# Sliding-window and linear attention side by side: v's weights loaded by parts of the contraction, an output projection moved, and the last rows stored in halves

## The chip, the cores and the metric

The kernel runs on one core of a Trainium2 chip. The time is in device microseconds; the medians below are over three runs. The profile is of one further execution, whose own time stands beside its span. Engines are named as in the profile: PE multiplies matrices, PEld loads its weights, DVE, ACT and POOL work on vectors, SP issues the DMA transfers here.

## What is computed

Two attention blocks of the same size on two inputs of 2048 tokens by 640 columns, 32 heads of 20, all in bfloat16. A is softmax attention in which a query sees itself and the 255 tokens before it. B is linear attention with phi(t) = t + 1 for positive t and exp(t) otherwise. Their outputs stand side by side in the result's columns.

```
qkv = x @ wqkv                      # both
A: s = q k^T * 20**-0.5, masked to 0 <= i - j < 256
   o = softmax(s) v ;  out[:, 0:640]    = o @ wo
B: kv = sum_s phi(k) v^T ;  z = sum_s phi(k)
   o = phi(q) kv / (phi(q) z + 1e-6) ;  out[:, 640:1280] = o @ wo
```

## The kernel before

Tokens are worked on in four blocks of 512 (`SB`; `s` from 0 to 3), the contraction of 640 in five parts of 128 (`KT`). A *chain* (line 275) is the five matmuls that add these parts up in one PSUM bank. Four banks of PSUM are shared by all chains (tiles named `dense`), and the other four hold the scores (`S_ps`). A bank comes free when its result has been copied out, by `evac` (line 257), which gives the copy to ACT or DVE by a running count of their load, or by `phi` (line 284), in which ACT takes the exponential and DVE finishes two chains later.

**The start.** The first 512 tokens of A's x are loaded in two halves (`load_half`, line 172) and transposed on PE (`transposes`, line 175), with copies from PSUM on DVE and ACT. Matmuls on zeros (`warm_up`, line 191) run on PE meanwhile. SP issues, in this order (lines 932 to 939): x's first half; v's weights of the first 16 heads, then of the other 16 (`load_w`, line 153: all five parts of the contraction, 320 columns, so runs of 640 B); x's second half; the raw weights of q and of k, which DVE, ACT and POOL regroup into `wqk`; a transposing load of A's next block; a part of B's weights; a transposing load of B's first block. The first chains on PE make v (`v_proj`, line 419): eight of them, 128 tokens by 16 heads each, in the order of line 453. The first two need the first load of v's weights, the next two the second; after four chains `hook` (line 409) puts in the transposes of x's second half, and four more chains follow. Then q's and k's rows (`a_rows`, line 392) begin.

**The body.** `scores` (line 744) puts out score products on PE, their exponential on ACT and the window's selects on POOL; `values` (line 797) multiplies by v, and DVE transposes and divides. Between these tiles PE is filled with the other chains. They come from `plan`: `at(t0, t1, gen, n)` spreads `n` pieces of a generator over a stretch of due times, `fill_of` (line 1039) sorts them, and `take` draws as many as a running credit allows. So the due times set the order on PE; they are not microseconds. Each engine works in the order so written. The pieces that matter here:

- `b_q(s)` (line 658): B's queries, five chains with `phi`, and a transposing DMA for each (line 675).
- `b_merge` (line 635): the products of B's state with B's output weights, ten short chains of two matmuls of 320 columns, copied into `wB`.
- `quotients(s)` (line 713): for each 128 tokens DVE divides (line 723) and SP issues a transposing DMA into the tile `xA` (line 727).
- `a_out(s)` and `b_out(s)` (lines 871, 731): the output projections of A and B, both by `wo_proj` (line 482): four chains of 512 columns, then one bank with the last 128 columns of all four token groups, one store for the block.

In the profile matmuls `dense<-wo,oT` are A's outputs, `dense<-wB,xA` with 512 columns B's outputs, `dense<-wo,kv_T` the merges, `dense<-xB,wB` B's queries.

**The end.** A's last block is projected by `a_out_last` (line 890), in two chains of 320 columns for each 128 tokens: DVE copies the first half out, ACT the second, and one store per 128 tokens follows (line 905).

Of the kernel before, what the change touches and what calls it, by code (L numbers as in the profile page):

```python
# [9 lines left out]
P = 128  # L10
# [7 lines left out]
DH = 20  # L18
HV = DH + 1
NG = H // 4  # L20
SB = 512
TPS = SB // P
# [70 lines left out]
def kernel(  # L93
# [10 lines left out]
    nc = tc.nc  # L104
    _, S, D = A_x.shape
    KT = D // P
# [3 lines left out]
    out2 = out[0]  # L110
# [29 lines left out]
    w_sb = {}  # L140
# [9 lines left out]
        "p (k n) -> p k n", n=D  # L150
    )

    def load_w(n, src, i, eng, lo=0, hi=D):
        wv = src.rearrange("(kt p) n -> p kt n", p=P)
        cols = slice(i * D + lo, i * D + hi)
        dst = w_sb[n][:, :, lo:hi] if n == "A" else w_sb[n][:, :, cols]
        eng.dma_start(out=dst, in_=wv[:, :, cols])

    xsrc = {"A": A_x[0], "B": B_x[0]}

    def load_x(n, s):
        t = xp.tile([P, KT, SB], BF16, name=f"x{n}")
        nc.sync.dma_start_transpose(out=t[:], in_=xsrc[n][s * SB : (s + 1) * SB, :])
        return t

    def load_x_first():

        tok = pqp.tile([P, TPS, D], BF16, name="phi")
        src = xsrc["A"][0:SB, :].rearrange("(t p) d -> p t d", p=P)
        t = xp.tile([P, KT, SB], BF16, name="xA")  # L170

        def load(i):
            nc.sync.dma_start(out=tok[:, 2 * i : 2 * i + 2, :], in_=src[:, 2 * i : 2 * i + 2, :])

        def transposes(i):
            for tb in (2 * i, 2 * i + 1):
                ps = dps.tile([P, 2 * SB], BF16, name="dense")
                for c in range(KT):
                    nc.tensor.transpose(
                        ps[:, c * P : (c + 1) * P], tok[:, tb, c * P : (c + 1) * P], ident[:]  # L180
                    )
                dst = t[:, :, tb * P : (tb + 1) * P]
                pv = ps[:, 0:D].rearrange("p (c q) -> p c q", q=P)
                if tb % 2:
                    nc.scalar.activation(out=dst, in_=pv, func=ACT.Copy)
                else:
                    nc.vector.tensor_copy(out=dst, in_=pv)

        return t, load, transposes

    def warm_up(wait):

        z = op.tile([P, TPS, D], BF16, name="osb")
        nc.vector.memset(z[:, 0, 0:P], 0.0)
        ps = dps.tile([P, SB], F32, name="dense")
        for n in wait:
            for _ in range(n):
                nc.tensor.matmul(
                    ps[:, 0:P], lhsT=z[:, 0, 0:P], rhs=z[:, 0, 0:P], start=True, stop=True
                )  # L200
            yield
# [27 lines left out]
    def flush(before=None):  # L229

        while later and (before is None or later[0][0] <= before):
            later.pop(0)[1]()
# [9 lines left out]
    def settle(all=True):  # L242
        while posts and (all or posts[0][0] <= begun[0]):
            posts.pop(0)[1]()
# [12 lines left out]
    def evac(dst, src, n=SB, to=None):  # L257

        if to is None:
            to = "A" if load["A"] < load["D"] + AHEAD else "D"  # L260
        load[to] += n + COPY
        if to == "A":
            nc.scalar.activation(out=dst, in_=src, func=ACT.Copy)  # L263
        else:
            nc.vector.tensor_copy(out=dst, in_=src)  # L265

    def bank(wide=False):
        flush(begun[0] - 2)
        begun[0] += 1
        settle(False)  # L270
        if wide:
            return dps.tile([P, 2 * SB], BF16, name="dense")
        return dps.tile([P, SB], F32, name="dense")

    def chain(dst, lhs, rhs, n):

        for kt in range(KT):
            nc.tensor.matmul(  # L278
                dst, lhsT=lhs(kt), rhs=rhs(kt), start=(kt == 0), stop=(kt == KT - 1)
            )  # L280
            if kt < KT - 1:
                yield n
# [23 lines left out]
    def banks(g, n):  # L306

        for _ in range(n):
            for c in g:
                yield c  # L310
                if isinstance(c, End):
                    break

    xA, xB = {}, {}
    q_pad, k_pad, v_tok = {}, {}, {}
# [7 lines left out]
    for c in range(KT):  # L323
        m = EXTRA * c
        while m < EXTRA * (c + 1):
            n = min(EXTRA * (c + 1) - m, DH - m % DH)
# [12 lines left out]
    def regroup(i, src, heads, extras):  # L339

        def four(g):
            return src[:, :, 4 * DH * g : 4 * DH * (g + 1)].rearrange("p k (j d) -> p k j d", d=DH)

        for c in range(KT):
            dst = wqk[:, i, :, c * P : (c + 1) * P].rearrange("p k (j e) -> p k j e", e=32)
            heads(dst[:, :, :, 0:DH], four(c))
            for _, row, g, d, n in [piece for piece in pieces if piece[0] == c]:
                extras(dst[:, :, :, row : row + n], four(g)[:, :, :, d : d + n])
# [10 lines left out]
    def in_turn(*fns):  # L359
        n = [0]  # L360

        def copy(dst, src):
            n[0] += 1
            fns[n[0] % len(fns)](dst, src)

        return copy
# [39 lines left out]
                moves(n, s, pad)  # L406
            yield End(SB)

    def hook(gen, n, fn):

        for i, c in enumerate(gen):
            if i == n:
                fn()
            yield c

    hh = H // 2
    by_tokens = [(tb, i) for tb in range(TPS) for i in range(2)]

    def v_proj(n, xt, dst, order=by_tokens):
        v0 = 0 if n == "A" else 2 * D  # L420
        for tb, i in order:
            ps = bank()
            yield from chain(
                ps[:, 0 : hh * DH],
                lambda kt: xt[:, kt, tb * P : (tb + 1) * P],
                lambda kt: w_sb[n][:, kt, v0 + i * hh * DH : v0 + (i + 1) * hh * DH],
                hh * DH,
            )
            evac(
                dst[:, tb, i * hh : (i + 1) * hh, 0:DH],  # L430
                ps[:, 0 : hh * DH].rearrange("p (h d) -> p h d", d=DH),
                hh * DH,
            )
            yield End(hh * DH)

# [2 lines left out]
    v_bufs = [t[:, 0:VW].rearrange("p (t h e) -> p t h e", h=H, e=HV) for t in v_flat]  # L440
# [7 lines left out]

    def a_v(s):
        v_tok[s] = v_bufs[s % 3]  # L450
        order = by_tokens
        if s == 0:
            order = [(0, 0), (1, 0), (0, 1), (1, 1), (2, 0), (2, 1), (3, 0), (3, 1)]
        yield from v_proj("A", xA[s], v_tok[s], order)

    def tok_rows(xt, wt, base, done):

# [432 lines left out]
    def a_out_last(s):  # L890
        settle()
        osb = op.tile([P, TPS, D], BF16, name="osb")
        for tb in range(TPS):
            for lo, hi, to in ((0, D // 2, "D"), (D // 2, D, "A")):
                ps = bank()
                for _ in chain(
                    ps[:, 0 : hi - lo],
                    lambda kt: oT_A[s][:, kt, tb * P : (tb + 1) * P],
                    lambda kt: wo_sb["A"][:, kt, lo:hi],
                    hi - lo,  # L900
                ):
                    pass
                evac(osb[:, tb, lo:hi], ps[:, 0 : hi - lo], to=to)
            r0 = s * SB + tb * P
            nc.sync.dma_start(out=out2[r0 : r0 + P, 0:D], in_=osb[:, tb, :])


    def run(gen):
        for _ in gen:
            pass  # L910
# [18 lines left out]
        )  # L929

    xA[0], load_half, transposes = load_x_first()
    load_half(0)
    load_w("A", A_wqkv, 2, nc.sync, 0, hh * DH)
    load_w("A", A_wqkv, 2, nc.sync, hh * DH, D)
    load_half(1)
    raw = [load_raw(i) for i in range(2)]
    xA[1] = load_x("A", 1)
    load_w("B", B_wqkv, 1, nc.sync)
    xB[0] = load_x("B", 0)
    a_v0 = a_v(0)  # L940
    dummies = warm_up((28, 3))
    next(dummies)
    transposes(0)
    next(dummies)
    run(hook(banks(a_v0, 6), 4 * KT - 1, lambda: transposes(1)))
    regroup(0, raw[0], dve_copy, in_turn(act_copy, pool_copy))
    run(a_v0)
    regroup(1, raw[1], in_turn(dve_copy, act_copy), in_turn(act_copy, pool_copy))
# [34 lines left out]
    def at(t0, t1, gen, n):  # L983
        for i in range(n):
            plan.append((t0 + (i + 0.5) / n * (t1 - t0), gen, i == n - 1))
# [37 lines left out]
        at(td, td + 0.1, b_den(s), 1)  # L1023
        do(tx, tx, [lambda s=s: quotients(s)])
    at(46.5, 54, b_merge(), 2 * KT)
    for n, s, t0, t1 in (("A", 0, 44.5, 48.5), ("A", 1, 51.5, 55.5), ("B", 0, 55.5, 59.5),
                         ("B", 1, 60.2, 64), ("A", 2, 64.4, 68.2), ("B", 2, 69, 73),
                         ("B", 3, 73, 76)):
        at(t0, t1, (a_out if n == "A" else b_out)(s), KT)
# [35 lines left out]
    for i, (s, parts, selects, done) in enumerate(units):  # L1065
        p = scores(s, parts, selects)
# [6 lines left out]
        if ready and ready[0][0] + LAG <= i:  # L1073
# [3 lines left out]
            _, at = ready.popleft()  # L1077
# [10 lines left out]
    while ready:  # L1088
        take(5500)
        _, at = ready.popleft()  # L1090
# [3 lines left out]
    for _ in fill:  # L1094
        pass
    flush()
    a_out_last(NS - 1)

# [28 lines left out]
```

## Time and profile before

| | us |
|---|---|
| median of three runs (lowest, highest) | 262.4 (262.16, 262.49) |
| time of the profiled execution | 262.3 |
| its span, first to last instruction | 260.6 |
| PE busy | 252.0 (97%) |
| ACT busy | 200.5 (77%) |
| DVE busy | 175.3 (67%) |
| POOL busy | 172.7 (66%) |

The busy time of PE is an average over the whole span, and PE works at the granted full clock (0.998). PE stands before about 1 us, in the first 11 us, in a few places in the body and after the last matmul. Matmuls are pipelined: the next one starts before the one before has ended, so spacing between starts is shorter than the mean duration of one (a 320-column matmul shows 300 ns, and ten of them take 1.52 us). A line of the timeline gives its start, its length, the engine, the line of the kernel, the instruction and its tiles (output <- inputs), its shape, how many there were, and in brackets how long the engine was idle before it and what ended that.

### The profile page before, as it was taken

The numbers are of one execution on the slowest core, as the hardware profiler recorded it, in microseconds if no ns is written. First come the engines' busy times: TensorE is split into PE (matmuls) and PEld (weight loads), VectorE is DVE, ScalarE is ACT, GpSimd is POOL, SyncE is SP. The second block draws the span as 40 slices with busy tenths as digits, with TensorE's granted clock in tenths as the row PEclk, the third lists the DMA queues.
The fourth block names the chain that finished last, engine by engine and source line by source line (L and its number), as shares of the span: only waits on it lengthen the run. The fifth ranks groups of instructions, "written<-read, shape, count | busy, mean of one in ns | idle before, by whom it ended". The sixth has DMA issues, their size and how long they took to land.

```text
span 260.6 us, 10806 instructions
## 1 busy us (share of the span) xinstructions
PE 252.0 (97%) x4769; PEld 142.2 (55%) x4769; DVE 175.3 (67%) x307; ACT 200.5 (77%) x261; POOL 172.7 (66%) x211
## 2 busy tenths in 40 slices
PE   8699999999999999999999999999999999999995
PEld 7444445556455745555457555556445554555573
DVE  0344787786745457876646677699896887979752
ACT  3366888899767788988667887789879988978642
POOL 6114777777795866758495778949576694977800
PEclk9999999999999999999999999999999999999999
DMA  6998578699458892403474692633976596573724
GB/s 193 304 253 160 80 203 127 118 290 209 85 82 257 133 288 40 144 3 62 98 103 128 72 170 47 170 38 69 183 100 159 96 188 148 89 154 78 232 55 173
DMA packets 65508, 36.35 MB, mean 140 GB/s; under 512 B 48181, under 2 KB 64437, under 8 KB 65461
## 3 DMA queue, kind: packets, MB, share of 16 engines
q1 hardware_dynamic: 65461, 35.67, 64.3%
q8 instruction: 37, 0.61, 1.0%
q14 instruction: 10, 0.08, 0.1%
HBM read 14.42 MB, written 9.83 MB: 93 GB/s over the span
## 4 chain that ended last, share of the span: by engine, by line
PE 82%; POOL 6%; DVE 5%; DMA 3%; ACT 2%; issue 1%; SPq 0%; DVEq 0%; ACTq 0%
PE dense L278 52%; PE S_ps L754 10%; PE dense L537 10%; PE dense L813 8%; POOL p L786 4%; DMA wA<-in_A_wqkv_dram 3%; POOL plow L786 2%; ACT p L772 1%; DVE phi L295 1%; DVE e L292 1%; DVE tok L723 1%; PE dense L616 1%; PE dense L644 1%; PE dense L687 1%; ACT e L288 1%
## 5 line engine op out<-in xcount | busy, mean ns | idle before, releaser
L772 ACT ACTIVATE p<-S_ps 128x2048 bf16<-128x2048 f32 x76 | 142.3, 1872 | 34.5 <-PE S_ps L754 33.6
L786 POOL TENSOR_SCALAR_AFFINE_SELECT p<-p 128x512 bf16<-128x512 bf16 (+1 forms) x152 | 123.7, 824 | 63.8 <-ACT p L772 58.5
L278 PE MATMUL dense<-xA,wqk 128*128 128x512 bf16 x200 | 50.0, 380 | 0.0
L786 POOL TENSOR_SCALAR_AFFINE_SELECT plow<-p 128x1024 bf16<-128x1024 bf16 x32 | 39.2, 1225 | 2.2
L278 PEld LDWEIGHTS <-xA 128*128 128x128 bf16 x320 | 26.5, 98 | 20.6 <-issue 3.9
L754 PE MATMUL S_ps<-qpad,kpad 20*64 20x64 bf16 (+3 forms) x1728 | 35.2, 213 | 0.0
L754 PEld LDWEIGHTS <-kpad 20*64 20x64 bf16 (+1 forms) x1728 | 17.4, 100 | 29.4 <-issue 24.7
L826 DVE STREAM_TRANSPOSE T<-dense 128x512 f32<-128x512 f32 x32 | 22.8, 712 | 14.7 <-PE dense L813 14.7
L292 DVE TENSOR_SCALAR e<-e 128x512 bf16<-128x512 bf16 x40 | 22.5, 562 | 12.7 <-ACT e L288 12.2
L278 PE MATMUL dense<-wA,xA 128*128 128x320 bf16 x160 | 27.6, 300 | 2.3 <-DMA wA<-in_A_wqkv_dram 2.0
L278 PEld LDWEIGHTS <-wqk 128*128 128x128 bf16 x200 | 18.5, 98 | 20.6 <-issue 1.3
L295 DVE SCALAR_TENSOR_TENSOR phi<-dense,e 128x512 bf16<-128x512 f32 x40 | 27.7, 691 | 1.5
L813 PE MATMUL dense<-p,vA 128*32 128x64 bf16 (+2 forms) x1152 | 27.1, 223 | 0.6 <-POOL p L786 0.6
L278 PE MATMUL dense<-xB,wB 128*128 128x512 bf16 x100 | 25.4, 380 | 0.6 <-DVE phi L295 0.6
L288 ACT ACTIVATE e<-dense 128x512 bf16<-128x512 f32 x40 | 23.5, 594 | 3.2 <-PE dense L278 3.0
L278 PE MATMUL dense<-wB,xB 128*128 128x512 bf16 (+1 forms) x160 | 25.9, 300 | 0.0
L278 PE MATMUL dense<-wo,oT 128*128 128x512 bf16 (+2 forms) x160 | 25.1, 300 | 0.6 <-DVE wB L265 0.6
L537 PE MATMUL dense<-phi,tok 128*128 128x512 bf16 (+1 forms) x160 | 25.1, 300 | 0.2 <-DVE phi L295 0.2
L278 PE MATMUL dense<-wB,xA 128*128 128x512 bf16 (+1 forms) x160 | 24.6, 300 | 0.0
L813 PEld LDWEIGHTS <-vA 128*32 128x32 bf16 x1664 | 22.2, 96 | 3.6 <-issue 1.5
L843 DVE TENSOR_TENSOR N<-T,recA 128x320 bf16<-128x320 f32 (+1 forms) x28 | 18.3, 653 | 3.6 <-DMA oT<-N 2.7
L263 ACT ACTIVATE osb<-dense 128x512 bf16<-128x512 f32 (+1 forms) x23 | 12.8, 567 | 6.9 <-PE dense L278 6.7
(67 smaller groups left out, 229.4 us busy)
## 6 DMA issues: line engine op xcount, KB each, us to landing
out_dram<-osb SPq DMA_DIRECT2D x7, 640.0 KB
x_scr<-xB SPq DMA_DIRECT2D x4, 640.0 KB
tok<-in_B_x_dram SPq DMA_DIRECT2D x4, 640.0 KB
xB<-x_scr SPq DMA_DIRECT2D x4, 640.0 KB
wB<-in_B_wqkv_dram SPq DMA_DIRECT2D x3, 800.0 KB
q_scr<-qpad SPq DMA_DIRECT2D x16, 60.0 KB
k_scr<-kpad SPq DMA_DIRECT2D x16, 60.0 KB
qpad<-q_scr SPq DMA_DIRECT2D x16, 60.0 KB
```

Of the source, the lines that this page charges most:

```text
L263: nc.scalar.activation(out=dst, in_=src, func=ACT.Copy)
L278: nc.tensor.matmul(dst, lhsT=lhs(kt), rhs=rhs(kt), start=(kt == 0), stop=(kt == KT - 1))
L288: nc.scalar.activation(out=view(e), in_=src, func=ACT.Exp)
L292: nc.vector.tensor_scalar(out=e[:], in0=e[:], scalar1=1e-6, scalar2=1.0 + 1e-6, op0=ALU.add, op1=ALU.min)
L295: nc.vector.scalar_tensor_tensor(out=dst, in0=src, scalar=0.0, in1=view(e), op0=ALU.max, op1=ALU.add)
L537: nc.tensor.matmul(out, lhsT=lhs(x, pk)[:, tb, :], rhs=rhs(pk, tb), start=(i == 0), stop=(i == len(blocks) - 1),)
L754: nc.tensor.matmul(columns(S_ps[k0:k1], j, col, n, step), lhsT=kt[32 * j : 32 * j + DH, g, ko + k0 : ko + k1], rhs=q_pad[s][32 * j : 32 * ...
L772: nc.scalar.activation(out=p, in_=S_ps[:], func=ACT.Exp, scale=scale)
L786: nc.gpsimd.affine_select(out=dst, in_=src, pattern=[[0, 4], [0, n // HALF], [sgn, HALF]], compare_op=ALU.is_ge, fill=0.0, base=base, chan ...
L813: nc.tensor.matmul(O_ps[32 * j : 32 * (j + 1), q0 : q0 + n], lhsT=v_flat[kb // TPS % 3][:, at + j * HV : at + j * HV + 32], rhs=columns(p, ...
L826: nc.vector.transpose(out=T.rearrange("p b e -> p (b e)"), in_=O_ps[:])
L843: nc.vector.tensor_tensor(out=dst[:, :, at : at + b - a], in0=T[:, :, a - lo : b - lo], in1=r[:].to_broadcast([P, SB // 32, b - a]), op=AL ...
```

## The change

Three places change; the two input loads and all other code stay as they are.

1. v's weights come in two loads of whole rows (640 columns, 1280 B): contraction parts 0 and 1, then 2 to 4, in place of two halves of the columns. The first four chains of v (`v_abreast`, new) are open at once in four banks: parts 0 and 1 of each, then parts 2 to 4 of each, with the copy out as each one ends. The transposes of x's second half follow, and the other four chains as before. `hook` is gone.
2. In the plan A's second output (`a_out(1)`) has due times 49.2 to 54.2 in place of 51.5 to 55.5, and B's first output 55.2 to 59.4 in place of 55.5 to 59.5. The merges keep 46.5 to 54.
3. The last 128 rows of A's last block are stored in two DMAs of 320 columns, each after its own copy; the three row groups before them in one DMA each as before.

```diff
-    def load_w(n, src, i, eng, lo=0, hi=D):
+    def load_w(n, src, i, eng):
         wv = src.rearrange("(kt p) n -> p kt n", p=P)
-        cols = slice(i * D + lo, i * D + hi)
-        dst = w_sb[n][:, :, lo:hi] if n == "A" else w_sb[n][:, :, cols]
-        eng.dma_start(out=dst, in_=wv[:, :, cols])
+        cols = slice(i * D, (i + 1) * D)
+        eng.dma_start(out=w_sb[n][:, :, cols], in_=wv[:, :, cols])
...
+    def v_product(ps, xt, tb, i, kt):
+        nc.tensor.matmul(
+            ps[:, 0 : hh * DH],
+            lhsT=xt[:, kt, tb * P : (tb + 1) * P],
+            rhs=w_sb["A"][:, kt, i * hh * DH : (i + 1) * hh * DH],
+            start=(kt == 0),
+            stop=(kt == KT - 1),
+        )
...
+    def v_abreast(xt, dst, order, k0):
+        pss = [bank() for _ in order]
+        for ps, (tb, i) in zip(pss, order):
+            for kt in range(k0):
+                v_product(ps, xt, tb, i, kt)
+        for ps, (tb, i) in zip(pss, order):
+            for kt in range(k0, KT):
+                v_product(ps, xt, tb, i, kt)
+            v_rows(ps, dst, tb, i)
...
-            r0 = s * SB + tb * P
-            nc.sync.dma_start(out=out2[r0 : r0 + P, 0:D], in_=osb[:, tb, :])
+                r0 = s * SB + tb * P
+                if tb == TPS - 1:
+                    nc.sync.dma_start(out=out2[r0 : r0 + P, lo:hi], in_=osb[:, tb, lo:hi])
+                elif hi == D:
+                    nc.sync.dma_start(out=out2[r0 : r0 + P, 0:D], in_=osb[:, tb, :])
...
+    K0 = 2
+    wv = A_wqkv.rearrange("(kt p) n -> p kt n", p=P)
     load_half(0)
-    load_w("A", A_wqkv, 2, nc.sync, 0, hh * DH)
-    load_w("A", A_wqkv, 2, nc.sync, hh * DH, D)
+    for k0, k1 in ((0, K0), (K0, KT)):
+        nc.sync.dma_start(out=w_sb["A"][:, k0:k1, :], in_=wv[:, k0:k1, 2 * D : 3 * D])
     load_half(1)
...
-    run(hook(banks(a_v0, 6), 4 * KT - 1, lambda: transposes(1)))
+    v_tok[0] = v_bufs[0]
+    v_abreast(xA[0], v_tok[0], by_tokens[0:4], K0)
+    transposes(1)
+    a_v0 = v_proj(xA[0], v_tok[0], by_tokens[4:])
+    run(banks(a_v0, 2))
...
-    for n, s, t0, t1 in (("A", 0, 44.5, 48.5), ("A", 1, 51.5, 55.5), ("B", 0, 55.5, 59.5),
+    for n, s, t0, t1 in (("A", 0, 44.5, 48.5), ("A", 1, 49.2, 54.2), ("B", 0, 55.2, 59.4),
```

`v_rows` is the copy that ended each chain before: `evac` of the chain's 320 columns into v's tile.

More of the change, by code (lines that the diff above doesn't have):

```diff
@@ L407, in a_rows, with v_rows, v_proj @@
             yield End(SB)
[L409 to L414, printed above, removed]
     hh = H // 2
     by_tokens = [(tb, i) for tb in range(TPS) for i in range(2)]
-    def v_proj(n, xt, dst, order=by_tokens):
-        v0 = 0 if n == "A" else 2 * D
+    def v_product(ps, xt, tb, i, kt):
[6 more added lines that the diff above has]
+        )
+    def v_rows(ps, dst, tb, i):
+        evac(
+            dst[:, tb, i * hh : (i + 1) * hh, 0:DH],
+            ps[:, 0 : hh * DH].rearrange("p (h d) -> p h d", d=DH),
+            hh * DH,
+        )
+    def v_proj(xt, dst, order):
         for tb, i in order:
             ps = bank()
[L423 to L433, printed above, removed]
-            yield End(hh * DH)
+            for kt in range(KT):
+                v_product(ps, xt, tb, i, kt)
+                if kt < KT - 1:
+                    yield hh * DH
+            v_rows(ps, dst, tb, i)
+            yield End(hh * DH)
+    def v_abreast(xt, dst, order, k0):
[5 more added lines that the diff above has]
+            for kt in range(k0, KT):
+                v_product(ps, xt, tb, i, kt)
+            v_rows(ps, dst, tb, i)
     VW = TPS * H * HV
@@ L450, in a_v @@
         v_tok[s] = v_bufs[s % 3]
[L451 to L454, printed above, removed]
+        yield from v_proj(xA[s], v_tok[s], by_tokens)
     def tok_rows(xt, wt, base, done):
@@ L939 @@
     xB[0] = load_x("B", 0)
-    a_v0 = a_v(0)
     dummies = warm_up((28, 3))
```

## The prediction

> **What bounds the kernel now.** I read section 1 of the page first: PE is busy 252.0 of 260.6 us, so only the 8.6 us in which PE stands can be won while its work stays the same, and it does (4769 matmuls before and after, of the same shapes). Next came PE's waits, then the chain of waits in the first 14 us, then the timelines of PE and DVE around each wait. PE's waits over the whole span, the three that this change can touch (total us, times, longest):
>
> ```profile
> PE dense L278 <- DMA wA<-in_A_wqkv_dram: 2.0, 2, 1.7
> PE dense L278 <- DVE phi L295: 0.6, 1, 0.6
> PE dense L278 <- DVE wB L265: 0.6, 1, 0.6
> ```
>
> The first is at the start. The chain there (start, us, what) shows one load of v's weights, issued at 1.82, that lands after 6.52 us, then ten matmuls that it let go, x's transposes and their copies, and the rest of v:
>
> ```profile
> 1.82 6.52 DMA wA<-in_A_wqkv_dram
> 8.35 0.04 issue
> 8.39 1.52 PE dense L278 x10
> 9.90 0.29 PE dense L179 x5
> 10.20 0.02 issue
> 10.22 0.50 DVE xA L187
> 10.72 0.05 issue
> 10.77 3.32 PE dense L278 x22
> ```
>
> From 10.77 on PE has no wait of over 0.3 us until 185, so what the start gives reaches the end. The other two waits stand in PE's timeline, before the lines that end in brackets; DVE's timeline shows what they waited for:
>
> ```profile
> 184.64 0.98 PE L644 MATMUL dense<-wo,kv_T 120*128 120x320 bf16 x6
> 186.23 1.24 PE L278 MATMUL dense<-wo,oT 128*128 128x512 bf16 x5 [0.60 <-DVE wB L265]
> 192.03 0.65 PE L687 MATMUL dense<-zk,phi 128*128 128x8 bf16 x20
> 193.32 1.24 PE L278 MATMUL dense<-xB,wB 128*128 128x512 bf16 x5 [0.65 <-DVE phi L295]
> ```
>
> ```profile
> 184.50 1.27 DVE L723 TENSOR_TENSOR tok<-tok,rden 128x640 bf16<-128x640 bf16 x1
> 185.69 0.48 DVE L265 CAST wB<-dense 128x320 bf16<-128x320 f32 x1
> 192.58 0.69 DVE L295 SCALAR_TENSOR_TENSOR phi<-dense,e 128x512 bf16<-128x512 f32 x1
> ```
>
> Three merges (L644, two matmuls each) stand one after another; each fills a PSUM bank that must be copied out, and A's second output (L278, wo,oT) waits until the copy of the second merge, behind a 1.27 us multiplication on DVE, ends at 186.17.
>
> **The change, part by part.** The sum is made against the profiled run's own time, 262.3 us: its span of 260.6 and 1.7 around it. The median of the runs is 262.4.
>
> *The start.* Before, two halves of the columns (410 KB each, 640 B runs) fed four chains: the first half ten matmuls, the second ten. Now the contraction parts 0 and 1 come first (328 KB, 1280 B runs), then 2 to 4 (492 KB), and all four chains finish only after the second load. So after the second landing there are 12 matmuls, not 10: at 1.52 / 10 = 0.15 us each, +0.30. The eight that go ahead run from about 5.04, when DVE's first copy of x has ended (4.50 + 0.49), to 6.2, under the wait; the first load, which held PE 0.22 us at 5.12, is smaller and no longer ends that wait. Break-even is thus a second landing 0.30 us sooner, at 8.05.
>
> When does it land? The windows, us by us, give 254 to 282 GB/s from 4 to 7 and 346 to 384 from 8 to 11. In the trace's packet records a 640 B packet takes 32 ns and a 1280 B packet 55 ns, so an engine's share (80 packets before, 40 now) takes 2.56 and 2.20 us: 0.36 sooner. But bandwidth is not what is late: by the trace's landings 9 of the 16 DMA engines had brought the second half by 6.21, 11 by 6.59, the last only at 8.35, and x's second half repeats that lag (first 6.79, last 9.21). Between 4.3 and 6.5 single packets took 230 to 680 ns. Without the lag the landing is near 6.0, with all of it 8.35 - 0.36 = 8.0; the ends are 6.0 and 8.35 (nothing gained). The 1280 B packets of B's weights show stalls of 300 to 940 ns at 15.3 to 16.3, so long runs aren't spared, and I take 7.95: -0.1. At 6.0 the eight matmuls would end last, and x's second half and the raw weights that DVE and POOL regroup would be sooner by much the same: 8.35 - 6.2 - 0.30 = 1.85 won. At 8.35 the start costs 0.30.
>
> The Trainium skill (DMA: Bandwidth & Descriptors, Specifications) puts the least transfer for line rate at 512 B, by which 640 B runs lose nothing and doubling them wins nothing; the windows and packets above show a difference, if a small one. By the rule the start costs 0.30 instead of giving 0.1, which is a rival below.
>
> Four chains abreast need four banks; the trace has the last one free at 5.48 (ACT's copy of x, 4.78 + 0.70), before the third chain needs that copy's data anyway. Their evacuations keep their order on ACT and DVE; two are done before x's transposes reuse the banks: nothing. The regrouping starts at the raw weights' landing (POOL at 11.51), q's rows on PE at 13.50, some 0.1 us of slack on DVE: nothing at a shift of 0.1.
>
> *A's second output between the merges.* No instruction is added or dropped; PE's order changes between 184.64 and 214. Worked by hand from the durations of before and the waits of the built program: the output's first chain takes the bank that the transpose T freed at 183.34 and starts at 184.64; it takes 1.09 (the b_q chain of the same size at 189.00 is followed by the next matmul at 190.09). Two merges (0.27 each) run to 186.27. The next chain needs the first of these merges' bank: its copy starts at 186.1 on DVE (free at 185.77) and ends at 186.58, so PE stands 0.3 to 0.4 us instead of 0.60. From there the chains alternate with scores and values, and the banks come back in time. The second wait was for phi of the b_q chain just before, with little PE work between; now that chain ends at 192.25, its exp on ACT at 193.1, phi at 194.5, and PE gets to the next b_q chain at about 194.4: 0.1 instead of 0.65. From the profile's waits that is 1.25 - 0.45 = 0.8 won; counted from the issue spacing (six merges end at 185.46, the wait is 0.77; the other 0.80) it is 1.57 - 0.49 = 1.1. I take 1.0. Ends: 0 (the stalls move to other banks) and 1.25 + 0.3, if the POOL wait at 213.57 (0.32) goes as well.
>
> What is late next? b_out(0) starts at 202.23, some 1.1 sooner now. It reads the fourth transposed piece of B's first output; its issue on SP was at 196.01 and its landing at 199.86. Now xB's reload and the tok transpose ahead of it change places, and the fourth quotient on DVE comes after A's last transpose (191.42 + 0.71), at about 192.4 instead of 190.5; SP gets to the piece at about 195.9 as before, so it lands by 200 and is read at 201.1. A's output store goes ahead of three transposes, which are issued 0.54 later each (SP has nothing from 197.24 to 200.14). The selects on POOL for the values at 197.7 had ended at 196.7; now 196.0 against a need at 197.0. All three covers hold, the narrowest by 1 us. oT of the second block was complete near 131, 50 us ahead.
>
> *The last rows in halves.* SP issues the last store at 257.92, packets run from 258.75 to 259.34, the end is at 260.6. Each engine has eight packets of 1280 B (0.44 us); a half has eight of 640 B (0.26): -0.18. The added first half is ready at 257.27 (DVE's cast, 256.78 + 0.49) and its issue of 0.33 ends before 257.90, when ACT ends. Ends 0 and -0.2; I take -0.1, as packets of one engine can overlap a little.
>
> Sum: 262.3 - 0.1 - 1.0 - 0.1 = 261.1.
>
> **Rivals.** *The lag goes with the short runs* (0.13): 8 of the 11 packets of over 200 ns from 4.3 to 6.5 were 640 B ones; against it are the stalled 1280 B packets. Then up to -1.85 at the start: 262.3 - 1.85 - 1.1 = 259.35, or half of it, 260.3.
>
> *The length of the runs buys nothing* (0.15): the second landing stays at 8.35, 12 matmuls follow: 262.3 + 0.3 - 1.1 = 261.5. The unchanged bytes and the lag of the last engines speak for it, the 32 and 55 ns against. It is what the line-rate rule of the Trainium skill (DMA: Bandwidth & Descriptors, Specifications) would give here.
>
> *The stalls between the merges move, and don't go* (0.14): ACT is 77% busy and DVE has work at all times in 180 to 194; osb's copy of 512 columns takes 0.60 on ACT where a merge's took 0.41, just ahead of an exp. Then the start and end alone count: 262.3 - 0.2 = 262.1, no difference.
>
> *Slower* (0.08): b_out(0) waits for the last piece of its operand. From 201.1 each us of lateness is a us of PE, which runs in order, and past 202.4 it outweighs all that is won. SP has eight transposes from 185.84 to 197.24, 1.2 to 2.4 each; with three more of 1.25 ahead of the piece it lands at 199.9 + 3.75 = 203.65 and PE stands 2.55: 261.1 + 2.55 = 263.65. Against it: in SP's order the same transposes stand ahead of the piece as before.
>
> **The numbers.** The forecast has 0.50. Time 261.1. The low end takes half of the lag's rival (260.3 less its spread): 259.9; the high end takes the run-length rival and the moved stalls at 262.1: 262.2. What is left out is some 0.08 below and 0.1 above. No change means within 0.2%, 0.5 us of 262.4, about what a measurement tells apart: 261.9 to 262.9. Faster: nearly all of the forecast (0.48), both start rivals (0.13 + 0.14) and a little of the moved stalls (0.02): 0.77. Same: the rest of these, 0.16. Slower: 0.07.
>
> **What would show it.** A second wA wait that ends near 8.0, then twelve L412 matmuls; the wait for phi near 193 gone or under 0.2, that for wB at about 186 near 0.35; b_out(0) at 201 without a DMA wait; the last store's packets over 0.2 us sooner after its issue. A second landing past 8.5, or a DMA wait ahead of b_out(0), would make the forecast wrong.

## The result, and the profile after

The changed kernel takes 261.1 us (median of 16 runs, 260.12 to 262.18), the kernel before 262.1 beside it on the same chip (16 runs, 261.53 to 262.74): a ratio of 0.996 with a 95% interval of 0.9946 to 0.9974, so 0.7 to 1.4 us sooner. The forecast was 261.1. The profiled execution took 261.33 us with a span of 259.6; that of before, 262.3 and 260.6.

PE's waits over the whole span, after (total us, times, longest):

```profile
PE dense L412 <- DMA wA<-in_A_wqkv_dram: 1.8, 1, 1.8
...
PE dense L277 <- DVE wB L264: 0.3, 1, 0.3
```

Of the three waits that the change could touch, that for phi ahead of B's queries is gone, that for `wB` has halved, and that for v's weights is nearly as long as it was. The chain of waits in the first 14 us, after (start, us, what):

```profile
1.82 6.68 DMA wA<-in_A_wqkv_dram
...
8.54 1.79 PE dense L412 x12
10.33 0.29 PE dense L178 x5
...
10.65 0.50 DVE xA L186
...
11.20 2.89 PE dense L412 x20
```

The second load of v's weights landed at 8.50, not at the 7.95 taken, and twelve matmuls follow it in 1.79 us. PE is back in its long stretch at 11.20, 0.43 later than before. The order between the merges, PE's timeline after, the merges being L652 (start, us, engine, line, what, shape, count, idle before it and what ended that):

```profile
185.07 1.24 PE L277 MATMUL dense<-wo,oT 128*128 128x512 bf16 x5
186.15 0.71 PE L652 MATMUL dense<-wo,kv_T 120*128 120x320 bf16 x4
187.17 0.59 PE L277 MATMUL dense<-wo,oT 128*128 128x512 bf16 x2 [0.31 <-DVE wB L264]
...
194.78 0.65 PE L695 MATMUL dense<-zk,phi 128*128 128x8 bf16 x20
195.29 1.24 PE L277 MATMUL dense<-xB,wB 128*128 128x512 bf16 x5
...
201.60 1.03 PE L277 MATMUL dense<-wB,xA 128*128 128x512 bf16 x4
```

And what DVE did for them, its timeline after:

```profile
184.93 1.27 DVE L731 TENSOR_TENSOR tok<-tok,rden 128x640 bf16<-128x640 bf16 x1
186.63 0.49 DVE L264 CAST wB<-dense 128x320 bf16<-128x320 f32 x1 [0.42 <-PE dense L652]
...
194.30 0.69 DVE L294 SCALAR_TENSOR_TENSOR phi<-dense,e 128x512 bf16<-128x512 f32 x1
```

A's output now starts at 185.07, two merges follow, and the next chain stands 0.31 us for the copy that ends at 187.12. The B query at 195.29 carries no bracket: phi had ended at 194.99. B's first output starts at 201.60 without a wait for its operand; before it was at 202.23.

At the end, the timeline of all engines after:

```profile
256.56 0.95 SPq L914 DMA_DIRECT2D out_dram<-osb  x2
256.72 0.44 ACT L262 ACTIVATE osb<-dense 128x320 bf16<-128x320 f32 x1 [0.92 <-PE dense L277]
```

ACT's last copy ends at 257.16 (256.72 + 0.44) and the span at 259.62, 2.46 later. Before, the two were 257.90 and 260.60:

```profile
257.46 0.44 ACT L263 ACTIVATE osb<-dense 128x320 bf16<-128x320 f32 x1 [0.92 <-PE dense L278]
```

So between these two executions the start lost 0.43, which still stands at 182 (182.30 to 182.73); by ACT's last copy PE's work is 0.74 sooner, so the middle gave 1.17; and the end gave 0.24. Together -0.98, which is the difference of the spans (-1.0).

### The profile page after: what moved, and what is told of

Read it like the earlier page. It is cut to its first block, busy times and chain, and to the rows that moved or that the text cites. A ratio compares the mean times of both kernels' runs of the same rounds, so it can differ in the third digit from the quotient of the medians.

```text
span 259.6 us, 10761 instructions
## 1 busy us (share of the span) xinstructions
PE 247.7 (95%) x4722; PEld 142.4 (55%) x4769; DVE 177.0 (68%) x308; ACT 200.3 (77%) x260; POOL 171.8 (66%) x211
## 4 chain that ended last, share of the span: by engine, by line
PE 80%; POOL 6%; issue 4%; ACT 3%; DVE 3%; DMA 3%; SPq 0%; ACTq 0%; DVEq 0%
PE dense L277 43%; PE S_ps L762 10%; PE dense L545 9%; PE dense L821 8%; PE dense L412 7%; POOL p L794 4%; DMA wA<-in_A_wqkv_dram 3%; ACT p L780 2%; POOL plow L794 2%; PE dense L652 1%; PE dense L695 1%; DVE phi L294 1%; ACT e L287 1%; PE dense L624 1%; DVE e L291 1%
## 5 line engine op out<-in xcount | busy, mean ns | idle before, releaser
L277 PE MATMUL dense<-xA,wqk 128*128 128x512 bf16 x183 | 47.2, 379 | 1.1 <-issue 0.6
L277 PE MATMUL dense<-wB,xB 128*128 128x128 bf16 (+1 forms) x156 | 25.4, 297 | 0.8 <-issue 0.6
L277 PE MATMUL dense<-wo,oT 128*128 128x128 bf16 (+2 forms) x154 | 24.3, 296 | 1.0 <-issue 0.6
L545 PE MATMUL dense<-phi,tok 128*128 128x128 bf16 (+1 forms) x154 | 24.3, 296 | 0.7 <-issue 0.3
L277 PE MATMUL dense<-xB,wB 128*128 128x512 bf16 x90 | 24.2, 380 | 0.6 <-issue 0.3
L277 PE MATMUL dense<-wB,xA 128*128 128x512 bf16 (+1 forms) x156 | 23.4, 297 | 0.5 <-issue 0.3
L412 PEld LDWEIGHTS <-xA 128*128 128x128 bf16 x160 | 14.3, 98 | 11.2 <-issue 3.1
L731 DVE TENSOR_TENSOR tok<-tok,rden 128x640 bf16<-128x640 bf16 x16 | 19.8, 1238 | 0.0
```

The lines of the kernel that those rows point to most:

```text
L277: nc.tensor.matmul(dst, lhsT=lhs(kt), rhs=rhs(kt), start=(kt == 0), stop=(kt == KT - 1))
L412: nc.tensor.matmul(ps[:, 0 : hh * DH], lhsT=xt[:, kt, tb * P : (tb + 1) * P], rhs=w_sb["A"][:, kt, i * hh * DH : (i + 1) * hh * DH], start ...
L545: nc.tensor.matmul(out, lhsT=lhs(x, pk)[:, tb, :], rhs=rhs(pk, tb), start=(i == 0), stop=(i == len(blocks) - 1),)
L731: nc.vector.tensor_tensor(out=vh, in0=vh, in1=rden_of[s][:, tb, :, :].to_broadcast([P, H, DH]), op=ALU.mult)
```

## The experiments

Each edit is against the kernel before unless it says otherwise. Ratios are to the kernel before, run beside them (262.12, 262.01 and 262.18 us in the three sets). They are given as recorded, with their 95% intervals; they are not the quotients of the medians, which differ from them by a little over 0.1% at most.

**The start alone** (`start_alone`, and the same kernel again as `start_again`): the two loads by parts of the contraction and the four chains abreast; the old due times, the last rows in one store.

```diff
+    K0 = 2
+    wv = A_wqkv.rearrange("(kt p) n -> p kt n", p=P)
     load_half(0)
-    load_w("A", A_wqkv, 2, nc.sync, 0, hh * DH)
-    load_w("A", A_wqkv, 2, nc.sync, hh * DH, D)
+    for k0, k1 in ((0, K0), (K0, KT)):
+        nc.sync.dma_start(out=w_sb["A"][:, k0:k1, :], in_=wv[:, k0:k1, 2 * D : 3 * D])
...
-    run(hook(banks(a_v0, 6), 4 * KT - 1, lambda: transposes(1)))
+    v_tok[0] = v_bufs[0]
+    v_abreast(xA[0], v_tok[0], by_tokens[0:4], K0)
+    transposes(1)
+    a_v0 = v_proj(xA[0], v_tok[0], by_tokens[4:])
+    run(banks(a_v0, 2))
```

> Before with the start alone changed. By the two traces the start now costs: the second load lands at 8.50 and twelve matmuls follow it, so 0.3 to 0.5 us slower than before (ratio about 1.0015). By the forecast 0.1 us faster. If the parts only work together, something else.

> The start alone once more, on the chip of these runs. If the start is even in the mean (12 matmuls after an earlier landing), within 0.3 us of before; if it costs 0.3 to 0.5 us as the first profile of the changed kernel showed, ratio 1.0015. The second landing should lie between 6.6 and 8.5, as in the five profiles so far.

262.04 and 262.17 us (12 runs each), ratios 1.001 (0.9991 to 1.0029) and 1.0003 (0.9992 to 1.0014): no gain that shows. The second load landed at 7.18 in the one profiled execution and at 7.92 in the other. Both stalls between the merges are there, as PE's waits of `start_alone` show:

```profile
PE dense L277 <- DVE phi L294: 0.6, 1, 0.6
PE dense L277 <- DVE wB L264: 0.6, 1, 0.6
...
PE dense L412 <- DMA wA<-in_A_wqkv_dram: 0.4, 1, 0.4
```

This profiled execution took 261.38, the shortest of its twelve; its wait of 0.4 for the weights is not the usual one.

**The due times alone** (`plan_alone`).

```diff
-    for n, s, t0, t1 in (("A", 0, 44.5, 48.5), ("A", 1, 51.5, 55.5), ("B", 0, 55.5, 59.5),
+    for n, s, t0, t1 in (("A", 0, 44.5, 48.5), ("A", 1, 49.2, 54.2), ("B", 0, 55.2, 59.4),
```

> Before with the due times alone changed. By the traces and by the forecast the gain is here: 1.0 to 1.2 us faster (ratio about 0.996), PE's waits at 186 and 193 gone but for some 0.3 us. If the stalls only move, within 0.2 us of before.

261.25 us (12 runs), ratio 0.9974 (0.9959 to 0.9988). Of the three parts it alone is faster by a measurable amount, 0.3 to 1.1 us by that interval. PE's timeline in this kernel:

```profile
184.71 1.24 PE L278 MATMUL dense<-wo,oT 128*128 128x512 bf16 x5
186.81 0.59 PE L278 MATMUL dense<-wo,oT 128*128 128x512 bf16 x2 [0.31 <-DVE wB L265]
...
194.91 1.24 PE L278 MATMUL dense<-xB,wB 128*128 128x512 bf16 x5
```

The wait of 0.31 and the missing bracket at 194.91 are those of the changed kernel. Its second load landed at 8.43, so none of this came from the start.

**The halves alone** (`halves_alone`).

```diff
-            r0 = s * SB + tb * P
-            nc.sync.dma_start(out=out2[r0 : r0 + P, 0:D], in_=osb[:, tb, :])
+                r0 = s * SB + tb * P
+                if tb == TPS - 1:
+                    nc.sync.dma_start(out=out2[r0 : r0 + P, lo:hi], in_=osb[:, tb, lo:hi])
+                elif hi == D:
+                    nc.sync.dma_start(out=out2[r0 : r0 + P, 0:D], in_=osb[:, tb, :])
```

> Before with the last store alone in halves. By the forecast 0.1 us faster, by the trace of after up to 0.26 us; the stretch from ACT's last copy to the end of the span 2.7 us before, 2.45 here. If the extra store holds SP or the queue, 0 or slower.

261.78 us (12 runs), ratio 0.9993 (0.9978 to 1.0008): the times alone don't tell it from nothing. Its trace does: from the end of ACT's last copy to the end of the span there are 2.47 us, and 2.70 to 2.72 in the five profiled executions with one store for the last rows.

**All but the start** (`plan_and_halves`): the changed kernel with the old loads and the old order of v's chains, the diff of the start above turned round.

> The changed kernel with the start of before. If the start costs 0.4 us and the parts add up, 1.35 us faster than before, which is 0.4 us better than the changed kernel; by the forecast 1.1 us faster, no better than the changed kernel.

260.79 us (11 runs), ratio 0.996 (0.9945 to 0.9975), the ratio of the changed kernel. So the start adds nothing that can be measured; the median of 260.79 against 261.1, which comes from another set of runs, lies, if anything, on the side of a small loss.

**Is it the transposing load that holds the weights back?** (`held_after` and `held_old_start`, both with the new due times and the halves, the one with the new start, the other with the old.) SP issues the transposing load of A's next block at 4.45 us before and at 4.01 after, just when the weights are under way. A memset of its tile on POOL (5.14 to 7.38), for which it has to wait, puts off its issue to 7.41. Against the changed kernel:

```diff
         t = xp.tile([P, KT, SB], BF16, name=f"x{n}")
+        if n == "A":
+            nc.gpsimd.memset(t[:], 0.0)
         nc.sync.dma_start_transpose(out=t[:], in_=xsrc[n][s * SB : (s + 1) * SB, :])
```

> The changed kernel; the transposing load of A's second block waits for a memset of its tile on POOL (from about 5.2 to 7.5 us). If that load's issue at 4.0 us makes the DMA engines lag, v's second load lands near 6.2 instead of 8.5, PE restarts some 1.8 us sooner and the kernel is up to 1.8 us faster than the changed one. If the lag is the loads' own, the landing stays at 8.3 to 8.5 and the time within 0.3 us of the changed kernel.

> The start of before with the same hold, with the new due times and the halved last store. If the transposing load makes the lag, the second half of v's weights lands near 6.2 instead of 8.35 and ten matmuls follow; if not, it stays at 8.35. With the lag gone, the run length alone tells: 640 B runs should land 0.36 us later than the 1280 B runs of the run beside it, or at the same time if the length buys nothing.

260.94 (9 runs, ratio 0.9954, 0.9937 to 0.997) and 260.89 (7 runs, 0.9954, 0.9935 to 0.9972). With the old start the second load landed at 8.52 although no transposing load was issued before 7.41: 11 of its 16 engines had landed by 6.24, the next came at 6.96. With the new start it landed at 7.33. PE's waits of `held_old_start`:

```profile
PE dense L280 <- DMA wA<-in_A_wqkv_dram: 1.0, 1, 1.0
```

The idea that the transposing load makes the last engines late fell: the hold doesn't bring the landing forward beyond its usual spread, and the time of 260.94 is that of the changed kernel in the same set (261.07, below). The two starts are even here too.

**The changed kernel and the one before once more** (`after_again`, `before_again`), to see how much one kernel's landing moves.

> The changed kernel on the same chip as the three above: 1.0 us faster than before (ratio 0.996), second landing 8.3 to 8.6.

> The kernel before against itself: ratio 1.000, its interval is the noise of such a comparison. Second landing 8.0 to 8.5, as in all five profiles of the old start.

The changed kernel: 261.07 us (12 runs), ratio 0.9956 (0.9941 to 0.9971). Its second load landed at 6.62 in this profiled execution, against 8.50 in the first one, and that execution took 259.83, the shortest of its twelve. The kernel before against itself: 262.04 (12 runs), ratio 0.9996 (0.9982 to 1.001), landing at 8.49; its interval of 0.0014 to either side, 0.37 us, is about what such a comparison can't see.

**More matmuls under the wait** (`three_first`, again as `three_again`): against the changed kernel the first load holds three parts of the contraction, so twelve matmuls go ahead of the second landing and eight follow.

```diff
-    K0 = 2
+    K0 = 3
```

> The changed kernel with contraction parts 0 to 2 in the first load and 3 and 4 in the second. The second landing should stay at 8.5 (same bytes ahead of it); eight matmuls follow instead of twelve, so PE restarts 4 x 0.15 = 0.6 us sooner: 0.6 us faster than the changed kernel. If the first load now lands so late that its twelve matmuls run into the second landing (after 6.7 us), less.

> Parts 0 to 2 first, once more: 1.6 to 2.0 us faster than before (ratio 0.9925 to 0.994), 0.6 to 0.9 us faster than the changed kernel.

260.19 us (6 runs, ratio 0.9922, 0.9901 to 0.9943) and 259.61 (5 runs, ratio 0.9907, 0.9891 to 0.9923): 1.8 and 2.6 us under the kernel before by the medians, about 2.2, and so some 1.2 under the changed one; it is the fastest version of this study. The chain of waits in the first 14 us of `three_again`:

```profile
1.31 3.91 DMA wA<-in_A_wqkv_dram
...
5.26 2.75 PE dense L412 x18
...
9.14 2.89 PE dense L412 x20
```

The chain holds the first load, not the second: the twelve matmuls from 5.26 last until 6.9, the second landing comes at 6.98, and the thirteenth starts at 7.03, 0.13 later than it would have. PE is back in its long stretch at 9.14, against 11.20 and 9.46 in the two profiles of the changed kernel. `three_first` landed at 7.32, shows no wait of PE for the weights at all, and is back at 9.79. The 0.6 us that was expected of it counted four matmuls fewer behind an unchanged landing. In both profiles the second landing also came sooner than the 7.97 that is worked out for the changed kernel below; why it did, no run shows.

**And one more** (`four_first`).

```diff
-    K0 = 2
+    K0 = 4
```

> The changed kernel with contraction parts 0 to 3 in the first load and the last part alone in the second. If only the count of matmuls after the second landing matters, four follow it instead of eight, and it is 0.6 us faster than three_first. If the last engines' lag sits on whatever is fourth-fifths down the queue, the first load itself lands near 7 to 7.5, its sixteen matmuls (2.4 us) end at 9.5 to 10, and it is no faster than three_first or slower by up to 0.8 us.

260.7 us (12 runs), ratio 0.9952 (0.9933 to 0.9971): no better than two parts and worse than three. The chain of waits in the first 14 us:

```profile
1.31 4.45 DMA wA<-in_A_wqkv_dram
...
5.80 2.99 PE dense L412 x17
...
8.88 0.45 ACT vA L262
9.33 0.04 issue
9.37 0.45 PE dense L178 x5
...
10.39 2.89 PE dense L412 x20
```

The first load is now four fifths of the bytes and lands at 5.76 in this execution, the second at 6.19. PE starts v at 5.80, 0.4 to 0.5 us later than at three parts (5.41 and 5.26), and there is no long wait left to cover; the transposes of x's second half then stand until ACT has copied v out (8.88 + 0.45). The nearer comparison is `three_first`, whose first matmuls ran as slowly (last section): PE is back in its long stretch at 10.39 here and at 9.79 there.

## Why the prediction was right, and where a step failed

The total was right for the mechanism that carried it. Of its three terms one had the wrong sign, or nearly, and the other two were too small. That the time came out to the tenth is luck: the sum started from 262.3, and the kernel before had a median of 262.1 in these runs, so 1.2 us were forecast and 1.0 measured.

**A's second output between the merges: right, -1.0 taken, -1.16 measured.** The time from the first score product on PE to the end of ACT's last copy leaves out the start and the end. It is 238.84 to 239.02 us in the five profiled executions with the old due times (before, both of the start alone, the halves alone, before again), and 237.69 to 237.97 in the nine with the new ones: means of 238.93 and 237.77. The steps came as worked out: a wait of 0.31 for `wB` (0.3 to 0.4 forecast), none for phi (0.1 forecast). Of the two ways of counting, the one by issue spacing (1.57 - 0.49) was the nearer. The time of `plan_alone` gives 0.3 to 1.1, a little less than the 1.16; by the working of the landings below its runs started 0.3 us later than the mean of the old start (8.50 against 8.16), which would make up for it. The wait for POOL late in the body stayed (0.27 at 212.89 after 0.32), so the further 0.3 of that end was rightly left out. The rivals "the stalls move" and "b_out(0) waits" both fall with these lines and with the time of `plan_alone`.

One step beside this term was misread: which chain of B's first output needs the fourth transposed piece. The prediction had it read where the output starts. In the kernel each chain reads the 128 tokens of its own `tb` (`tok_rows`), and the traces agree: in `plan_alone` the output starts at 201.22, before that piece has landed at 201.58. It is the fourth chain that needs it. In the changed kernel this chain starts at 207.93, with the sixth of the eight matmuls in this line of PE's timeline, and the piece was issued at 196.79 and landed at 201.38:

```profile
206.85 1.89 PE L277 MATMUL dense<-wB,xA 128*128 128x512 bf16 x8
```

So the cover is over 6 us, not the 1 forecast, and the rival "slower" had too early a point from which lateness would have cost anything.

**The last rows in halves: right in kind, -0.1 taken, -0.24 measured.** What failed is the discount, that packets of one engine "can overlap a little". From the issue of the last store to the end of its last packet there were 1.42 us before (257.92 to 259.34) and 1.24 after (257.18 to 258.42): the -0.18 worked out, in full. Another 0.06 came off the stretch behind the packets (1.26 before, 1.20 after), which no term held.

**The start: -0.1 forecast, -0.1 to +0.3 measured.** The comparisons that differ in the start alone read, by medians, -0.1 and 0.0 (`start_alone`, `start_again`), 0.05 (held) and 0.3 (the changed kernel against `plan_and_halves`, with equal ratios); none is clear of the 0.37 that such a comparison can't see. The count of matmuls was right, and the two more cost 0.27 (twelve in 1.79, ten in 1.52; 0.30 taken). The step that failed is the landing: "without the lag the landing is near 6.0, with all of it 8.35 - 0.36 = 8.0", and of these 7.95 was taken, as if the lag were a property of the kernel. It is one of the execution. With the old loads the second landing was at 8.35, 8.43, 8.27, 7.99, 8.49 and, held, 8.52; with the new ones at 8.50, 7.18, 7.92, 6.62 and, held, 7.33.

An execution's time moves with its landing about one to one: `start_alone` and `start_again` are the same kernel, with landings 0.74 apart and times 0.80 apart (261.38 and 262.18). It is not exact: the two profiles of the changed kernel have landings 1.88 apart and times 1.50 apart, because PE was back 1.74 sooner and the middle took 0.23 longer. So the landing that belongs to a kernel's median can be worked out from a profiled execution: 7.18 + (262.04 - 261.38) = 7.84 for `start_alone`, and likewise 7.91, 7.86 and 8.27 for `start_again`, `after_again` and the changed kernel, a mean of 7.97. For the old loads `before_again`, `plan_alone`, `halves_alone` and `plan_and_halves` give 7.96, 8.50, 7.97 and 8.22, a mean of 8.16. So the new landing was about the 7.95 forecast, but the old one is 0.2 sooner than the 8.35 of the one execution it was counted against. Sooner by 0.19, against 0.27 for two more matmuls behind it: a loss of about 0.1. This is an estimate worked out from the runs, not measured. The values of one start lie up to 0.5 apart, so a difference of 0.19 isn't clear of their spread; it does lie where the comparisons put it.

The rival in which the length of the runs buys nothing comes closest for this term. The windows of the changed kernel, us by us (start and end of the window, length, busy us and count of PE, PEld, DVE, ACT and POOL, granted clock, DMA share, GB/s), still show from 4 to 7 us no more than with 640 B runs, which moved 254 to 282 GB/s:

```profile
4.00:5.00 1.00, 1.00 (x13) 1.00 (x11) 0.20 (x1) 0.00 (x0) 1.00 (x1) 1.00 0.99 260
...
6.00:7.00 1.00, 0.75 (x5) 0.41 (x5) 0.00 (x0) 0.00 (x0) 0.00 (x0) 1.00 0.98 229
```

The last of these in the kernel before:

```profile
6.00:7.00 1.00, 0.64 (x5) 0.33 (x4) 0.00 (x0) 0.76 (x2) 0.00 (x0) 1.00 0.88 282
```

That doubling runs of 640 B raises no rate agrees with the line rate that the Trainium skill (DMA: Bandwidth & Descriptors, Specifications) puts at 512 B and above. What delays the landing is the lag: the share is near 1 while 229 GB/s move, and the 16 engines of one load end 2.85 us apart (5.65 and 8.50). The rival in which the lag goes with the short runs falls: whole rows landed at 8.50 too, and in that execution 16 packets of 1280 B took over 200 ns between 4.3 and 6.5 us, the longest 973, where before there were 11 of both lengths. Four of the five landings of the new start are sooner than all six of the old, but the median times of the two starts are even: three of the four (7.18, 6.62 and 7.33) belong to executions 0.7 to 1.2 us under their kernel's median.

**The sum.** With the terms as the traces give them, -1.16 and -0.24, the middle and the end are -1.4, and the changed kernel's -1.0 leaves +0.4 for the start, at the edge of what its own comparisons allow. The forecast's -1.2 came near because a term that was too good at the start met two that were too small. The prediction had also named a second landing past 8.5 as what would make it wrong; in the profiled execution it came at 8.50 and cost the 0.43 that the first chain shows, and the middle still outweighed it.

What makes the last DMA engines late, and more so in some executions, stays open. The transposing load's early issue was tried and is not it.

## What to carry to other kernels

A landing in a profile is one draw: before you count on half a us of it, look at the same load in several executions. Rather than make the load a little sooner, put enough work ahead of it that its spread is covered (three parts of five here; two left PE standing, and with four the first load itself came late). Chains that each end in a copy stall when they stand in a row; a longer chain whose operands are long ready, set between them, gives the copies their time, and here the order alone took 1.16 us off the middle of the traces. A last store in two halves, the first sent while the second is still being copied, shortened the tail by 0.24 us, of which 0.18 is the packets that no longer stand at the end.

## What was not expected of the hardware

The first matmuls of v ran at half their speed in some executions: 0.27 us from one to the next for 320 columns instead of 0.14, in `plan_and_halves` from 5.40 to 6.47 and in `three_first` from 5.41 to 6.47, not in `three_again`. The timelines of `plan_and_halves` and of `three_again`:

```profile
5.40 2.16 PE L278 MATMUL dense<-wA,xA 128*128 128x320 bf16 x10
```

```profile
5.26 3.01 PE L412 MATMUL dense<-wA,xA 128*128 128x320 bf16 x20 [0.37 <-DMA wA<-in_A_wqkv_dram]
```

Ten took 2.16 us in the one, twenty 3.01 in the other. The windows show a granted clock of 1.00 in both from 2 us on, but this column can mislead: the traces' own records of the granted clock begin, at full clock, only at 6.69 us in `plan_and_halves` and at 6.70 in `three_first`, just where the spacing falls to 0.14, and where there is no record the column reads 1.00. In `before` and the changed kernel, whose v has a spacing of 0.14 from its start (5.12 and 5.35), they begin at 3.75 and 5.04; `three_again` has none. The Trainium skill (TensorE: Matmul & The Clock Gate, "Part 1: The HAM clock gate") has a cold array at half clock, for a time that differs from run to run, with matmuls N / 1.2 GHz apart; that would be 0.267 us for 320 columns, an estimate from that page. The spacing agrees with it, and so does the place where the records begin.

Under a late landing this costs nothing; with three parts first it does, as the twelve matmuls are then what fills the wait: `three_first` was back in its long stretch at 9.79, `three_again` at 9.14.

The same load's last engine landed between 6.62 and 8.50 us in executions of one kernel, while its first landed at 5.56 and 5.65.
